# Two edits to the order of small work in a fused attention and rational feed-forward kernel: later normalisations, and stores and broadcasts issued ahead of weight transfers

## The chip, the core and the metric

The kernel runs on one core of one Trainium2 chip. The metric is the device time of one launch in microseconds (us), as the median of several runs. TensorE is written PE in the profile, its weight loads PEld; VectorE is DVE, ScalarE is ACT, GpSimd is POOL, and SyncE, which issues nearly all DMAs here, is SP.

## The reference

Attention over 4 batches and 8 heads with 576 positions and head size 64, with a learned bias on the distance of two positions, and then a feed-forward layer whose activation is a rational function. Cut to what matters:

```python
scores = scale * np.matmul(q, k.transpose(0, 1, 3, 2))
scores = scores + bias.transpose(2, 0, 1)[None, :, :, :]
scores = scores - np.max(scores, axis=-1, keepdims=True)
attn = np.exp(scores)
attn = attn / (np.sum(attn, axis=-1, keepdims=True) + 1e-09)
x = np.matmul(attn, v)                      # to 2304 tokens x 512
h = x @ w_in                                # 512 -> 2048
g = P(h) / (Q(h) + 1e-06)                   # two polynomials in h and |h|
return g @ w_out                            # 2048 -> 512
```

## The kernel before, in words

The work is done in two stages, and their instructions are put in order by hand: each engine executes what the program gives it in the order of the program, and the framework only adds the waits. That holds for SP too: a DMA whose wait isn't over holds up all DMAs behind it.

**Attention.** There are 16 units, a pair of heads of one batch each: unit u is pair u // 4 of batch u % 4. After a start in which the bias table is built, 72 steps handle 128 query rows (or, for the last 64 rows of two neighbouring units, a shared step) each, two steps to a round: round r (`rnd`, line 589) starts steps 2r and 2r + 1 and goes on with the steps of the rounds before. Within a round the order is:

- at the start, SP issues loads (`loads`), and DVE copies an output block of an earlier step from PSUM into the unit's tile `xs` (`puts`, line 494), then does the first part of a weights job;
- PE does the scores of both steps (`product`, line 340). DVE adds the bias and finds the maximum (`e_ttr`, line 356), ACT takes the exponential (line 372);
- PE transposes the probabilities of the two steps before (line 416), ACT copies them out (line 431), and PE multiplies them by v (line 485). The sums of the rows are collected on the way, and `put_tails` stores them to the DRAM tensor `rs` (lines 455 and 460);
- at the round's end stand the parts of the weights job that come last, the stores of finished units (line 402), the loads of the sums' reciprocals (line 388) and further loads.

**Normalisation.** The output of a unit is collected in `xs` without its division. The sums go to DRAM and come back as a broadcast over 64 partitions for each head, two DMAs into the tile `rb` (`load_rb`, line 385). `e_norm` (line 393) makes the multiply of the 128x576 tile (line 400), for most units on POOL, and the store to the DRAM tensor `xd` (line 402), which runs at the end of the round of the multiply. The tiles have few buffers: `rb` two and `xs` four, so that unit u + 2's broadcast waits for unit u's multiply, and unit u + 4's first copy into `xs` for unit u's store. `done_to` (line 533) says when a unit is due, by e, the step by which its last sums are under way (twice the round in which they go to DRAM): its broadcast is issued when step e is done with, and its multiply joins the list `norms` some steps later (line 542). A round takes one entry of that list, if one of its two POOL slots is free (lines 607 to 610): the slot `pool` ahead of the score passes, or `pool2` behind the second of them.

**Weights.** Beside the attention, 20 jobs split the weights into a high and a low part (`w_conv`, line 135, by the schedule of `job_plan`, line 559): a load of `wx` (line 139), DVE, ACT and POOL work (line 176 a POOL copy, line 180 a DVE join that waits for it, line 187 a POOL subtraction), and stores (lines 127 and 195). Two jobs take three rounds: the first of them fills `pool`, the second `pool2`, the third both, which are the rounds divisible by 3.

**Second stage.** From about 277 us on, the feed-forward runs over five tiles of tokens, twice, each half of the hidden size in turn. It reads the attention's output back from `xd` (`load_x`, line 284).

Of the kernel before, what the change touches and what calls it, by code (L numbers as in the profile page):

```python
# [37 lines left out]
def tile_attn_moe(  # L38
# [193 lines left out]
    with tc.manual_schedule():  # L232
# [3 lines left out]
        with ExitStack() as actx:  # L236
# [14 lines left out]
            def load_bias(p, c):  # L251
                if p not in bias:
                    bias[p] = bpool.tile([P, 10, S], F32, tag="bias", name=f"bias{p}")
                t = bias[p]
                r0, r1 = tab_rows(c, 2 * p), tab_rows(c, 2 * p + 1)
                for o, x, y, r in ((5 + c, 0, S, r1[:, 0:S]), (c, 64, S, r0[:, 0:512]), (c, 0, 64, r0[:, 512:S])):
                    n = P if c < 4 else 64
                    for z in range(0, P, n):
                        nc.sync.dma_start(out=t[z:z + n, o, x:y], in_=r)

            def load_qk(u, eng=nc.sync):
                p, b = units[u]
                t = qkp.tile([P, 2, S], F32, tag="qk", name=f"qk{u}", bufs=3)
                eng.dma_start(out=t, in_=qkt[b, p])
                qk[u] = (t[:, 0], t[:, 1])

            def load_v(u, eng=nc.sync):
                p, b = units[u]
                t = vpool.tile([P, 5, P], F32, tag="v", name=f"v{u}")
                eng.dma_start(out=t, in_=vp[b, p])  # L270
                vt[u] = t
# [4 lines left out]
            def load_x(n_, t, k0=0, k1=KD):  # L276
                if k0 == 0:
                    xr[n_] = xps[0].tile([P, KD, TM], F32, tag="xr", name=f"xr{n_}")
                x = xr[n_]
                d = 0  # L280
                while d < TS[t]:
                    b, o = divmod(T0[t] + d, S)
                    w = min(TS[t] - d, S - o)
                    nc.sync.dma_start(out=x[:, k0:k1, d:d + w], in_=xd[b][:, k0:k1, o:o + w])
                    d += w
# [40 lines left out]
            def side(i):  # L326
                return 4 * ((i // 2 - 1 + i) % 2) if i > 1 else 4
# [57 lines left out]
            def load_rb(u):  # L385
                t = rb[u] = npool.tile([P, S], F32, tag="rb", name=f"rb{u}")
                for j in range(2):
                    nc.sync.dma_start(
                        out=t[64 * j:64 * j + 64],
                        in_=rsum[u // 2][u % 2, j:j + 1, :].to_broadcast([64, S]),  # L390
                    )

            def e_norm(u):
                x = xs.pop(u)
                p, b = units[u]
                eng = V if u in (NX, NU - 1) else G
                f = rb.pop(u)

                def part(a, z):
                    op = eng.tensor_tensor(out=x[:, a:z], in0=x[:, a:z], in1=f[:, a:z], op=ALU.mult)  # L400
                    if z == S:
                        stores.append(lambda: nc.sync.dma_start(out=xd[b][:, p, :], in_=x))
                    return op

                return [lambda: part(0, S)]
# [59 lines left out]
            def weave(first, second):  # L465
                t = [0, 0]
                rest = [list(first), list(second)]
                while rest[0] or rest[1]:
                    r = int(not rest[0] or (bool(rest[1]) and t[1] < t[0]))
                    ns, op = rest[r].pop(0)  # L470
                    t[r] += ns
                    op()
# [28 lines left out]
            NS = len(steps)  # L501
            NU = len(units)
# [8 lines left out]
            def loads(i):  # L511
                g, c = divmod(i, UPG)
                for u, x, y in ((2 * g + 2, 0 if g else 4, 3 if g else 6), (2 * g + 3, 5 if g else 7, 8)):
                    if u < NU and c == x:
                        load_qk(u)
                    if u < NU and c == y and u != 3:
                        load_v(u)
                if i == UPG + 2:
                    load_v(3)
                p, r = divmod(i, 2 * UPG)  # L520
                r = {2: 0, 7: 1, 11: 2, 13: 3, 16: 4}.get(r)
                if r is not None and p + 1 < NP:
                    load_bias(p + 1, r)
                if i == NS - 18:
                    load_x(0, 0, 0, KD - 1)
                if i == NS - 5:
                    load_x(1, 1, 0, KD - 1)
# [5 lines left out]
            def done_to(k):  # L533
                for u in range(NU - 1):
                    e = 2 * full[u]
                    if k == (e if u < NX else e - 2):
                        load_rb(u)
                    if u == NX:
                        if k == NS - 8:
                            x12.append(xs[u])  # L540
                            late.extend(e_norm(u))
                    elif k == (NS if u == NU - 2 else min(e + 2 + u % 2 * 2, NS - 3)):
                        norms.extend(e_norm(u))

            def run(todo):
# [3 lines left out]
            def behind(x, y):  # L549
                tc.add_manual_dep(x.ins, y.ins.name, ORDER, reason="one at a time")  # L550
# [5 lines left out]
            def ended(*ks):  # L556
                return [steps[k][0] for k in ks if k >= 0 and last_of(k)]
# [31 lines left out]
            def rnd(r):  # L589
                i = 2 * r  # L590
                plan = job_plan(r)
                loads(i)
                op = None
                while puts:
                    op = puts.pop(0)()
                for x in plan["first"]:
                    op = x()
                for x in plan["act"]:
                    x()
                us = ended(i - 4, i - 3)  # L600
                sa, sb = e_qk(i), e_qk(i + 1)
                b, o = side(i), side(i + 1)
                ZZ = (o + 1, o + 3)
                main, ends, adds, copy = e_tp(i - 2, (b, b + 1), ZZ, us)
                main_, ends_, _, copy_ = e_tp(i - 1, (b + 2, b + 3), ZZ)
                weave(sa[0] + sb[0], sa[1] + sb[1])
                for k in ("pool", "pool2"):
                    if not plan[k] and norms:
                        plan[k].append(norms.pop(0))
                        break  # L610
                for x in plan["pool"]:
                    x = x()
                    if op is not None:
                        behind(x, op)
                e_ttr(i, 0, True)
                op = e_ttr(i, 1)
                for x in plan["between"]:
                    op = x()
                run(late)
                for x in plan["pool2"]:  # L620
                    behind(x(), op)
                small = [ends[r] + ends_[r] + adds[r] for r in range(2)]
                weave(main[0][:4] + small[0] + main[0][4:] + main_[0], main[1] + small[1] + main_[1])
                copy(1, 2)
                copy(0, 1)
                copy_(0, 2)
                for j in range(2):
                    e_ttr(i + 1, j)
                put_tails(i - 2, 2, ZZ, us)
                put = e_pv(i - 3, b + 1) if i > 2 else None  # L630
                puts.append(e_pv(i - 2, b))
                hi = split_x(0, (i - NS + 12) // 2) if i in (NS - 12, NS - 10, NS - 8) else ()
                if i == NS - 4:
                    hi = split_x(0, KD - 1, x12[0][:, :TS[0]])
                for x in hi[:1]:
                    x()
                for k in (i, i + 1):
                    for j in range(2):
                        e_exp(k, j)
                recip(i - 2)  # L640
                recip(i - 1)
                if put:
                    put()
                for x in plan["last"] + list(hi[1:]):
                    x()
                run(stores)
                done_to(i - 2)
                done_to(i - 1)
                loads(i + 1)
                if r == 2:  # L650
                    for x in jobs[:4]:
                        x[0]()
# [37 lines left out]
            with ExitStack() as bctx:  # L690
# [62 lines left out]
                for y, n in enumerate(order):  # L753
# [9 lines left out]
                    for a, z in zip(cuts, cuts[1:]):  # L763
                        b = pa[a // 512]
                        o = W[:, b, a % 512:a % 512 + z - a]
                        for c in range(4):
                            x = rows[n, c]
                            x = x[:, a - mid:z - mid] if a >= mid else x[:, mid - a:mid - z:-1]
# [4 lines left out]
                    e = rpool.tile([P, EW], F32, tag="e", name=f"e{n}")  # L773
# [9 lines left out]
                    g, k = divmod(n, 8)  # L783
# [310 lines left out]
```

## Time and profile before

| what | us |
| --- | --- |
| median of 3 runs | 660.6 (660.6 to 661.12) |
| the profiled execution | 661.6 |
| its span, first to last instruction | 659.8 |
| PE busy | 652.1 |
| DVE busy | 563.1 |
| ACT busy | 470.8 |
| POOL busy | 153.8 |

Times in the rows are microseconds from the start of the span. A row of the timeline gives the start, the length, the engine, the line, the operation and its tiles, the number of instructions that are merged in it, and in brackets the idle time of the engine ahead of it with what ended it. A q behind an engine's name means its sequencer, which issues DMAs. Busy shares are averages over stages with different limits; what a change is worth is read from the place where it acts.

### The profile page before, as it was taken

How to read it: one execution, taken by the hardware profiler on the slowest of the kernel's cores; microseconds unless marked ns; L12 is line 12 of the kernel's file. 1: busy time of each engine (PE TensorE's matmuls, PEld its weight loads, DVE VectorE, ACT ScalarE, POOL GpSimd, SP SyncE). 2: the span in 40 equal slices, each digit the busy share in tenths (PEclk: the TensorE clock that was granted, in tenths of full speed). 3: DMA queues.
4: the chain of work that ended last, by engine and by line, in shares of the span. 5: the costliest groups of instructions: out<-in, count | busy, mean ns of one | idle time of the engine just before them, and what ended most of it. 6: DMA issues, size and time to landing. Idle time of an engine off the chain costs nothing.

```text
span 659.8 us, 16141 instructions
## 1 busy us (share of the span) xinstructions
PE 652.1 (99%) x6276; PEld 549.6 (83%) x6276; DVE 563.1 (85%) x1102; ACT 470.8 (71%) x757; POOL 153.8 (23%) x108
## 2 busy tenths in 40 slices
PE   9999999999999999999999999999999999999997
PEld 7767888888888788988888888989988888888996
DVE  7997889998889895899999989979769779687776
ACT  7978999999899897767667566576655555555551
POOL 1000234333333331122222221222221221212211
PEclk9999999999999999999999999999999999999999
DMA  6899599788787674452835607669431301312031
GB/s 248 302 329 323 159 289 303 255 280 265 240 305 252 218 259 126 138 188 71 261 98 171 226 19 256 211 203 321 142 111 49 129 0 66 110 43 85 1 113 48
DMA packets 69901, 118.98 MB, mean 180 GB/s; under 512 B 9024, under 2 KB 30912, under 8 KB 69824
## 3 DMA queue, kind: packets, MB, share of 16 engines
q1 hardware_dynamic: 69680, 117.78, 53.9%
q8 instruction: 49, 0.80, 0.5%
q14 instruction: 28, 0.23, 0.1%
q10 hardware_dynamic: 144, 0.16, 0.1%
HBM read 79.17 MB, written 35.61 MB: 174 GB/s over the span
## 4 chain that ended last, share of the span: by engine, by line
PE 89%; DMA 4%; DVE 2%; ACT 2%; issue 1%; SPq 0%; POOL 0%; DVEq 0%; POOLq 0%
PE ps L313 30%; PE ps L922 30%; PE ps L485 10%; PE ps L340 9%; PE ps L769 6%; PE ps L416 5%; ACT p L372 1%; DMA rb<-rs 1%; DVE s L356 1%; DMA wx<-in_w_out_dram 1%; DMA ws<-wl 1%; ACT pt L431 1%; DVE ring L741 0%; DMA cst<-in_cst_dram 0%; POOL wl L187 0%
## 5 line engine op out<-in xcount | busy, mean ns | idle before, releaser
L892 POOL TENSOR_TENSOR gl<-m,r 128x1024 fp32r<-128x1024 f32 (+1 forms) x39 | 85.6, 2194 | 299.4 <-DVE m L885 262.3
L843 ACT ACTIVATE w<-ps,babs 128x1024 f32<-128x1024 f32 (+1 forms) x40 | 41.2, 1031 | 107.9 <-PE ps L313 104.2
L372 ACT ACTIVATE p<-s,m 128x576 f32<-128x576 f32 x144 | 110.1, 781 | 0.6 <-DVE m L356 0.6
L356 DVE CUSTOM_DVE_ANT_0 s<-ps,bias 128x576 f32<-128x576 f32 (+1 forms) x144 | 95.1, 681 | 6.8 <-PE ps L340 2.1
L431 ACT COPY pt<-ps 128x512 f32<-128x512 f32 (+1 forms) x109 | 71.7, 732 | 17.8 <-PE ps L416 17.8
L922 PE MATMUL ps<-woh,gh 128*128 128x512 f32 x216 | 84.3, 390 | 0.0
L922 PE MATMUL ps<-wol,gh 128*128 128x512 f32 x216 | 84.3, 390 | 0.0
L340 PE MATMUL ps<-qk 64*128 64x288 f32 (+1 forms) x640 | 81.7, 418 | 0.0
L855 DVE SCALAR_TENSOR_TENSOR u<-w,babs,ps 128x1024 f32<-128x1024 f32 (+1 forms) x40 | 46.9, 1172 | 38.2 <-ACT t L844 38.1
L485 PE MATMUL ps<-pt,v 128*64 128x128 f32 (+1 forms) x1280 | 78.5, 266 | 0.8 <-ACT pt L431 0.5
L485 PEld LDWEIGHTS ps<-pt,v 128*64 128x64 f32 x1280 | 65.3, 137 | 5.8 <-ACT pt L431 1.8
L313 PE MATMUL ps<-xb,wih 128*128 128x512 f32 (+1 forms) x240 | 68.8, 368 | 0.0
L850 ACT ACTIVATE u<-u 128x1024 f32<-128x1024 f32 (+1 forms) x40 | 39.1, 978 | 40.1 <-DVE u L855 40.0
L340 PEld LDWEIGHTS ps<-qk 64*128 64x128 f32 (+1 forms) x640 | 51.0, 176 | 19.5 <-issue 5.8
L416 PEld LDWEIGHTS ps<-ident,p 64*128 64x128 f32 x1296 | 50.3, 138 | 6.2 <-DVE m L356 0.5
L871 DVE SCALAR_TENSOR_TENSOR gh<-t,cst,r 128x1024 fp32r<-128x1024 f32 (+1 forms) x40 | 46.9, 1173 | 9.3 <-ACT r L852 6.9
L922 PE MATMUL ps<-woh,gl 128*128 128x512 f32 x216 | 53.8, 389 | 0.0
L416 PE MATMUL ps<-ident,p 64*128 64x64 f32 x1296 | 51.1, 226 | 0.1
L878 DVE SCALAR_TENSOR_TENSOR m<-u,qc,gh 128x1024 f32<-128x1024 f32 (+1 forms) x40 | 47.1, 1178 | 4.0
L313 PEld LDWEIGHTS ps<-xb,wih 128*128 128x128 f32 x240 | 44.6, 188 | 6.1
L885 DVE SCALAR_TENSOR_TENSOR m<-t,cst,m 128x1024 f32<-128x1024 f32 (+1 forms) x40 | 47.1, 1178 | 1.4
L864 DVE SCALAR_TENSOR_TENSOR t<-t,cst,ps 128x1024 f32<-128x1024 f32 (+1 forms) x40 | 47.0, 1174 | 1.4
(84 smaller groups left out, 1344.7 us busy)
## 6 DMA issues: line engine op xcount, KB each, us to landing
tab<-e SPq DMA_DIRECT2D x36, 295.5 KB
qk<-in_qkt_dram SPq DMA_DIRECT2D x16, 576.0 KB
wx<-in_w_in_dram SPq DMA_DIRECT2D x16, 512.0 KB
wx<-in_w_out_dram SPq DMA_DIRECT2D x16, 512.0 KB
v<-in_vp_dram SPq DMA_DIRECT2D x16, 320.0 KB
ws<-wh SPq DMA_DIRECT2D x20, 256.0 KB
ws<-wl SPq DMA_DIRECT2D x20, 256.0 KB
bias<-tab SPq DMA_DIRECT2D x16, 288.0 KB
```

The lines of the kernel that those rows point to most:

```text
L313: on(T.matmul(hps[s][:, j, :w_], w[:, k, sl], x[:, k, :w_], start=(k == 0 and z == 0), stop=(k == KD - 1 and z == 2),), b + j)
L340: on(T.matmul(W[o, b, :SH], q[r, x], k[r, a * SH:(a + 1) * SH], start=True, stop=True), b)
L356: op = on(V.tensor_tensor_reduce(out=t3[:, a], in0=W[:, b:b + 2][:, a, :SH], in1=b3[:, a], scale=-0.125, scalar=least, op0=ALU.add, op1=AL ...
L372: A.activation(out=prob[i][:, z * S:z * S + S], in_=t, func=AF.Exp, bias=m, scale=-1.0, accum_out=sums[u % 4][:, k:k + 1],)
L416: on(T.transpose(W[:, b, o:o + 64], src[x, :], ident[x, x]), b)
L431: on(A.copy(out=t.rearrange("p x (r s) -> p r x s", r=2)[:, a:z], in_=W[:, to[a]:to[a] + z - a].rearrange("p r (x s) -> p r x s", s=64),), ...
L485: on(T.matmul(ps[y, o], vt[n][:, kc, y], w_, start=(kc == 0), stop=(kc == 4)), b, mem=(f"pt{i % 3}", f"tl{i // 2 % 2}"))
L864: on(V.scalar_tensor_tensor(out=rt[s, "t"], in0=rt[s, "t"], scalar=abs_[:, 1:2], in1=hp(s), op0=ALU.add, op1=ALU.mult,), *hb(s), mem="t")
L878: V.scalar_tensor_tensor(out=m, in0=rt[s, "u"], scalar=qc, in1=rt[s, "gh"].bitcast(F32), op0=ALU.add, op1=ALU.mult,)
L885: V.scalar_tensor_tensor(out=m, in0=rt[s, "t"], scalar=abs_[:, 0:1], in1=m, op0=ALU.add, op1=ALU.subtract)
L892: eng.tensor_tensor(out=lo, in0=rt[s, "m"], in1=rt[s, "r0"], op=ALU.mult)
L922: on(T.matmul(po[n, c], l[:, j, c * P:(c + 1) * P], r[fp][:, j, :], start=(first and x is a), stop=(last and x is z),), OB[c])
```

## The change

Two edits. The first sets one due time for all normalisations that go through the common branch: e + 4, where units with an even number had e + 2 and units with an odd number e + 4. The second changes the order of calls at a round's end: the stores of finished units, then the broadcasts and due lists of `done_to`, and only then the last parts of the weights job.

```diff
--- before.py
+++ after.py
@@ -539,7 +539,7 @@
                         if k == NS - 8:
                             x12.append(xs[u])
                             late.extend(e_norm(u))
-                    elif k == (NS if u == NU - 2 else min(e + 2 + u % 2 * 2, NS - 3)):
+                    elif k == (NS if u == NU - 2 else min(e + 4, NS - 3)):
                         norms.extend(e_norm(u))
 
             def run(todo):
@@ -641,11 +641,11 @@
                 recip(i - 1)
                 if put:
                     put()
-                for x in plan["last"] + list(hi[1:]):
-                    x()
                 run(stores)
                 done_to(i - 2)
                 done_to(i - 1)
+                for x in plan["last"] + list(hi[1:]):
+                    x()
                 loads(i + 1)
                 if r == 2:
                     for x in jobs[:4]:
```

## Rows read from the trace of the kernel before

**Rows 1.** The page: engines' busy time, granted clock by slices, the chain that ended last

```profile
PE 652.1 (99%) x6276; PEld 549.6 (83%) x6276; DVE 563.1 (85%) x1102; ACT 470.8 (71%) x757; POOL 153.8 (23%) x108
...
PEclk9999999999999999999999999999999999999999
...
PE 89%; DMA 4%; DVE 2%; ACT 2%; issue 1%; SPq 0%; POOL 0%; DVEq 0%; POOLq 0%
```

**Rows 2.** The timeline of the ends of rounds 8 and 9, rounds 10 and 11

```profile
99.23 0.54 SPq L402 DMA_DIRECT2D xd<-xs  x1
...
101.55 0.46 SPq L139 DMA_DIRECT2D wx<-in_w_out_dram  x1
...
102.10 1.48 SPq L388 DMA_DIRECT2D rb<-rs  x2
...
103.64 1.53 SPq L259 DMA_DIRECT2D bias<-tab  x3
...
104.56 1.41 POOL L400 TENSOR_TENSOR xs<-xs,rb 128x576 f32<-128x576 f32 x1 [0.81 <-DVE m L356]
...
106.73 0.65 SPq L455 DMA_DIRECT2D rs<-rt  x1
...
107.58 2.37 PE L340 MATMUL ps<-qk 64*64 64x288 f32 x24
...
107.75 0.29 DVE L494 COPY xs<-ps 128x128 f32<-128x128 f32 x1 [0.19 <-issue]
...
108.71 0.79 PEld L340 LDWEIGHTS ps<-qk 64*128 64x128 f32 x8 [0.44 <-DVE wk L155]
...
113.45 2.21 PE L340 MATMUL ps<-qk 64*128 64x288 f32 x16
```

**Rows 3.** The timeline of round 20, with the broadcast issued ahead of it

```profile
153.87 1.68 SPq L388 DMA_DIRECT2D rb<-rs  x2
...
160.06 2.37 PE L340 MATMUL ps<-qk 64*64 64x288 f32 x24
...
162.63 1.41 POOL L400 TENSOR_TENSOR xs<-xs,rb 128x576 f32<-128x576 f32 x1 [4.17 <-DMA rb<-rs]
...
162.66 1.93 DVE L180 SCALAR_TENSOR_TENSOR wm<-wm,wh 128x512 uint32<-128x512 uint32 x1
...
166.77 2.21 PE L340 MATMUL ps<-qk 64*128 64x288 f32 x16
```

**Rows 4.** Line 180 over the whole span: count, least, median and longest ns

```profile
L180 DVE SCALAR_TENSOR_TENSOR wm<-wm,wh x20: 685/686/1932, 75.3 to 241.0; 128x512 uint32<-128x512 uint32 x20
```

**Rows 5.** The timeline of round 30

```profile
219.25 2.21 PE L340 MATMUL ps<-qk 64*128 64x288 f32 x16
...
219.62 1.42 POOL L400 TENSOR_TENSOR xs<-xs,rb 128x576 f32<-128x576 f32 x1 [7.84 <-DMA rb<-rs]
...
222.33 1.04 POOL L176 COPY wm<-wx 128x1024 uint16<-128x1024 uint16 x1
...
223.40 0.69 DVE L180 SCALAR_TENSOR_TENSOR wm<-wm,wh 128x512 uint32<-128x512 uint32 x1 [1.46 <-POOL wm L176]
...
225.70 0.34 PE L485 MATMUL ps<-tl,v 128*64 128x64 f32 x4 [1.22 <-DVE tl L443]
...
226.55 2.21 PE L340 MATMUL ps<-qk 64*128 64x288 f32 x16
```

**Rows 6.** The timeline of SP near the end of the attention, queue nearly empty

```profile
255.90 0.42 SPq L460 DMA_DIRECT2D rs<-rt  x1
257.22 1.11 SPq L388 DMA_DIRECT2D rb<-rs  x2
```

**Rows 7.** The windows: engines' busy us (count), granted clock, DMA share, GB/s

```profile
100.00:125.00 25.00, 24.95 (x434) 21.59 (x430) 22.61 (x78) 23.54 (x51) 9.47 (x8) 1.00 0.90 304
```

**Rows 8.** Line 720, the first matmuls, up to 4.6 us and from 4.8 us

```profile
L720 PE MATMUL ps<-warm x16: 421/422/582, 1.1 to 4.4; 128*128 128x128 f32 x16
...
L720 PE MATMUL ps<-warm x5: 274/276/421, 4.4 to 5.0; 128*128 128x128 f32 x5
```

## The prediction, made before the changed kernel was seen

> **What bounds the kernel now.** I read the page first, then the windows, then the timeline round by round. The page shows TensorE busy for 652.1 of 659.8 us, with 90% or more of its clock granted in every slice, and the chain that ended last is 89% TensorE [rows 1]. So nothing that the change does to DVE, ACT, POOL or the DMA queue counts by itself; it counts where TensorE waits for it, and only there. The attention rounds between 45 and 250 us are a strict beat: a round begins where the scores' matmuls (line 340) begin, and the plain one from 107.58 to 113.45 takes 5.87 us [rows 2]. Two rounds break the beat, and both by way of a normalisation on POOL. In round 20 the broadcast of unit 6's sums was issued at 153.87 to 155.55 and the multiply that reads it started only at 162.63; the DVE instruction of line 180 that started 0.03 us later took 1.93 us instead of its median 0.69, and the round took 166.77 - 160.06 = 6.71 us [rows 3, 4]. In round 30 unit 10's multiply, due in round 29, had waited 7.84 us for its broadcast; the weights' copy behind it on POOL started at 222.33, line 180 on DVE waited 1.46 us for that, TensorE 1.22 us behind it, and the round took 226.55 - 219.25 = 7.30 us [rows 5]. The reader should see in both that POOL is nearly idle and does harm only by being late.
>
> **Edit one, the due time (line 542).** Even units become due at e + 4 instead of e + 2, one round later; odd ones stay. A due normalisation is taken in the next round that leaves a POOL slot free, one each round, and rounds divisible by 3 leave none (both slots belong to weights). Worked through line 533 to 610: unit 0 goes from round 8 to 10, unit 1 from 10 to 11 (it queues behind unit 0), unit 2 from 11 to 13, 4 from 16 to 17, 6 from 20 to 22, 8 from 25 to 26, 10 from 29 to 31; the rest stay. The same 14 POOL multiplies run, so no busy time is added. What goes: both harmful ones now come two rounds after the old place, with the broadcast long landed. Round 20 gives back 6.71 - 5.87 = 0.84 us and round 30 gives 7.30 - 5.87 = 1.43 us, together 2.3 us. Next late would be DVE and ACT, but other rounds with a multiply in the same slot show that they keep the 5.87 us beat [rows 2].
>
> A later multiply also frees two buffers later, and this is the edit's price. The broadcast tile has two buffers: unit 2's broadcast, issued on SP at the end of round 9, needs unit 0's multiply done, which now is in round 10. SP issues in order, so everything behind that broadcast stands. The unnormalised output has four buffers: unit 4's first copy from PSUM (line 494, DVE, first thing in round 11) needs unit 0's store landed; that store was issued at 99.23 and is now issued at the end of round 10. I went through all later units: each has at least one round (5.8 us) between its store and the copy that wants the buffer, and unit 12's broadcast follows unit 10's multiply of the same round. Only round 11 collides.
>
> **Its size.** In round 10 the slot after the second score pass runs its multiply at 104.56, 1.41 us long, done at 105.97 [rows 2]; today that is unit 1's, then unit 0's. Only then does SP go on. With the lengths of today's rows it issues the two broadcasts 1.48, the next weights 0.46, three bias loads 1.53, the sums of unit 3 0.65: 4.12 us, to 110.1; then the store, 0.54 like today's, to 110.6 [rows 2]. Nothing shows a store's landing, so I bound it. Below: an unloaded issue that ended at 256.32 had landed when the broadcast that needs it was issued at 257.22, 0.9 us [rows 6]. Above: unit 6's broadcast needed 162.63 - 155.55 = 7.1 us under load [rows 3]. The queue will have run dry before 106, but then takes 1.7 MB in one burst (two 144 KB broadcasts, 512 KB, 576 KB, 4 KB, the store's 288 KB, by the shapes in the code); at the 304 GB/s of this stretch [rows 7] that alone is 5.6 us from 106, plus 0.9 twice: 113.4. I take the middle of the bounds, 4.0 us, as the byte count lies between: landed at 114.6, ends 111.5 and 117.7. The copy that ran at 107.75 starts there, 6.85 us late, and behind it on DVE stand the weights' mask and all score passes of the round. TensorE is no cover: half of the round's scores go to the bank that this copy empties, and it waited for DVE there already, 0.44 us until 108.71 [rows 2]. I allow 0.25 us for what it can still do: 6.6 us of stall, ends 3.2 and 9.7.
>
> **The clock behind the stall.** No row of before has TensorE idle for longer than about 1.2 us once at work, and that did not lower the granted clock [rows 1, 5]. The only rows after a long rest are the first: from 1.05 to about 4.6 us each 128x128 matmul took 0.42 us, with starts 0.21 us apart, then 0.28 us, starts 0.11 us apart: the 1.2 and the 2.4 GHz level [rows 8]. If the stall drops the clock, I expect the same again: some 3.6 us at half speed, 1.8 us lost; ends 0 and twice that. I take 1.8, as a rest of 6.6 us is nearer to the start's rest than to 1.2 us. The Trainium skill (TensorE: Matmul & The Clock Gate, "Part 1: The HAM clock gate") says that the half-rate clock is the default and that TensorE falls back to it after a stretch without work, which speaks against a change that opens such a hole. By that rule the result is 666.7 us, without it 664.9; no row here shows a fall in mid-kernel.
>
> **Edit two, the order at a round's end (lines 641 to 648).** Only SP's order changes: the DVE instructions among the moved calls have none of their own engine to pass. The store (one DMA) and the broadcast (two) go ahead of the weights' store or load. Where nothing waits that is worth at most the weights' issue, 0.3 to 1 us earlier for a transfer that now has two rounds to spare: nothing, hidden by that slack. Its price if the broadcast waits is that the weights' transfers stand behind it. In round 9 that is the load of job 7, wanted in round 14; in rounds 31 and 33, where the broadcast waits for its own sums, the last weights' stores, wanted in the second stage. All have whole rounds of cover: nothing. It also takes the high part's store out from in front of unit 0's store; that is why I didn't count it above.
>
> **Sum.** 6.6 + 1.8 - 2.3 = 6.1 us slower. The profiled execution took 661.6 us around its span of 659.8, 0.15% over the median of 660.6, so on the median: 666.7 us.
>
> **Rivals.** (a) *The stall is there and the clock stays up*: 660.6 + 6.6 - 2.3 = 664.9 us. For it: the clock never left full once it was reached [rows 1]. Against: it was never tried by such a rest. (b) *Faster: unit 0's store lands in time*. Place: round 11, DVE's first copy. It decides at 107.75: if SP did not stand at unit 2's broadcast, the store could be issued when the multiply ends, 105.97, take 0.54 and land 0.9 later, 107.4. Then only the 2.3 us count: 658.3 us. Against: two buffers, and a third broadcast ahead of the first one's reader in program order. (c) *The beat does not come back*: the moved multiplies meet line 180 elsewhere, as in round 20, and the 2.3 us are not gained: 669.0 us. Against: line 180's median of 0.69 us over 20 runs [rows 4] says that such a meeting is the exception. (d) *The stall is short*, near its lower end with no clock loss: 660.6 + 3.2 - 2.3 = 661.5 us, no change.
>
> **How the numbers follow.** Forecast 0.55, (a) 0.20, (b) 0.13, (c) 0.05, (d) 0.07. About 0.2%, 1.3 us, can be told from no change; so faster 0.13, same 0.07, slower 0.80. The forecast's own ends are 661.5 and 671.5 (9.7 + 3.6 - 2.3 = 11.0). The range leaves out (b), most of (d) and the last microsecond above: 662.0 to 670.5.
>
> **What would show it.** Round 11 lengthened by 6 to 9 us, with a DVE wait before the copy of line 494 that ends with the store of unit 0, and line 340 waiting on DVE; SP standing for some 5 us at line 388 until POOL's multiply ends near 106; a granted clock of half behind it; rounds 20 and 30 back to 5.8 to 5.9. I am wrong if round 11 keeps its beat, or if line 400 on POOL still waits some microseconds for a broadcast in rounds 20 to 31.

## The result, and the profile after

The changed kernel takes 667.78 us (667.56 to 668.59), the kernel before beside it 660.74 us: a ratio of 1.0108, with a 95% interval from 1.0090 to 1.0125, so 7.0 us slower. The forecast was 666.7 us, within 662.0 to 670.5. The two profiled executions differ by 6.0 us in their spans (665.8 and 659.8).

The page of the changed kernel has the same work and nearly the same busy times as [rows 1]; what is new is one slice in which TensorE falls to six tenths and the granted clock to eight:

```profile
PE 654.1 (98%) x6276; PEld 550.0 (83%) x6276; DVE 561.6 (84%) x1102; ACT 470.6 (71%) x757; POOL 153.5 (23%) x108
...
PE   9999996999999999999999999999999999999997
...
PEclk9999998999999999999999999999999999999999
```

It is the seventh of 40, from 99.9 to 116.5 us, and the place is round 11. Its timeline, which answers to [rows 2] line by line:

```profile
101.77 0.49 SPq L264 DMA_DIRECT2D qk<-in_qkt_dram  x1
...
104.75 1.41 POOL L400 TENSOR_TENSOR xs<-xs,rb 128x576 f32<-128x576 f32 x1 [0.81 <-DVE m L356]
...
106.19 1.15 SPq L388 DMA_DIRECT2D rb<-rs  x2
...
107.38 0.59 SPq L139 DMA_DIRECT2D wx<-in_w_out_dram  x1
...
107.76 1.20 PE L340 MATMUL ps<-qk 64*64 64x288 f32 x16
...
108.01 2.21 SPq L259 DMA_DIRECT2D bias<-tab  x3
...
110.32 0.65 SPq L455 DMA_DIRECT2D rs<-rt  x1
...
111.01 0.39 SPq L402 DMA_DIRECT2D xd<-xs  x1
...
114.73 0.29 DVE L494 COPY xs<-ps 128x128 f32<-128x128 f32 x1 [6.99 <-DMA xd<-xs]
...
115.08 1.46 PEld L340 LDWEIGHTS ps<-qk 64*128 64x128 f32 x8 [6.62 <-DVE xs L494]
115.08 2.29 PE L340 MATMUL ps<-qk 64*128 64x288 f32 x8 [6.12 <-DVE xs L494]
...
117.16 2.13 PE L416 MATMUL ps<-ident,p 64*128 64x64 f32 x36
...
121.76 2.21 PE L340 MATMUL ps<-qk 64*128 64x288 f32 x16
...
123.80 1.42 PE L416 MATMUL ps<-ident,p 64*128 64x64 f32 x36
```

It reads like a chain. POOL's multiply, now unit 0's, ends at 106.16. SP, which had ended its last issue at 102.26, only then issues unit 2's broadcast, and behind it all that had gathered: weights, bias, sums. Unit 0's store is issued at 111.01, where it was at 99.23 before. DVE's first copy of unit 4 has waited 6.99 us for it. TensorE has done the first step's scores (16 instructions, 1.20 us), needs the bank that this copy empties, and stands 6.1 us. Then its work takes longer: the 36 transposes 2.13 us against 1.42 us a round later. The windows (busy us of PE, PEld, DVE, ACT, POOL, then the granted clock, DMA share, GB/s) show why:

```profile
101.97:107.76 5.79, 5.79 (x96) 5.02 (x94) 5.24 (x18) 5.62 (x13) 2.45 (x2) 1.00 0.78 280
...
113.00:119.60 6.60, 4.52 (x48) 3.74 (x50) 4.37 (x14) 2.06 (x4) 2.70 (x2) 0.50 0.60 204
...
121.76:127.63 5.87, 5.87 (x115) 5.19 (x113) 4.77 (x17) 4.66 (x12) 2.32 (x2) 1.00 0.80 263
```

The granted clock is at full up to the stall, at half (1.2 GHz) from 113 to 119.6 us, and at full again in the next round. Round 11 takes 121.76 - 107.76 = 14.0 us instead of 5.87.

The rounds that should gain did. TensorE's timeline has round 20 at 174.24 - 168.36 = 5.88 us, against 6.71 [rows 3], and round 30 at 232.59 - 226.72 = 5.87 us, against 7.30 [rows 5]:

```profile
168.36 2.37 PE L340 MATMUL ps<-qk 64*64 64x288 f32 x24
174.24 1.97 PE L340 MATMUL ps<-qk 64*128 64x288 f32 x14
...
226.72 2.21 PE L340 MATMUL ps<-qk 64*128 64x288 f32 x16
232.59 1.73 PE L340 MATMUL ps<-qk 64*128 64x288 f32 x12
```

So the spans add up: 8.1 us lost in round 11, 0.8 and 1.4 won, 0.2 lost at the start, together 6.1 of 6.0 us.

### The profile page after: what moved, and what is told of

It reads as the page before. It is cut to its first block, busy times and chain, and to the rows that moved or that the text cites. A ratio compares the mean times of both kernels' runs of the same rounds, so it can differ in the third digit from the quotient of the medians.

```text
span 665.8 us, 16141 instructions
## 1 busy us (share of the span) xinstructions
PE 654.1 (98%) x6276; PEld 550.0 (83%) x6276; DVE 561.6 (84%) x1102; ACT 470.6 (71%) x757; POOL 153.5 (23%) x108
## 4 chain that ended last, share of the span: by engine, by line
PE 95%; ACT 2%; issue 1%; SPq 1%; DMA 1%; POOL 0%; DVE 0%; DVEq 0%; POOLq 0%
PE ps L313 30%; PE ps L922 30%; PE ps L485 12%; PE ps L340 11%; PE ps L769 6%; PE ps L416 6%; ACT p L372 1%; PE ps L720 1%; ACT pt L431 1%; DMA xd<-xs 1%; SPq L259 0%; POOL xs L400 0%; SPq L388 0%; DVE pre L943 0%; SPq L455 0%
```

## The experiments

My theory: the whole price lies in one place, unit 0's late multiply, by way of SP and the buffers of two tiles; the gain lies in late multiplies of units 6 and 10 and is worth having by itself. The rivals: the new order on SP costs, or later multiplies cost in general, or SP's standing costs by itself.

**One edit at a time.** The due time alone:

```diff
-                    elif k == (NS if u == NU - 2 else min(e + 2 + u % 2 * 2, NS - 3)):
+                    elif k == (NS if u == NU - 2 else min(e + 4, NS - 3)):
```

> The due time alone, with the old order at a round's end. My theory, that unit 4's first copy in round 11 waits for unit 0's store and that this store stands behind unit 2's broadcast on SP: round 11 takes 13.5 to 14.6 us, rounds 20 and 30 are plain at 5.8 to 5.9, the time is 667.5 to 668.5 us. Rival, that the new order on SP is what costs: no long round, 658 to 660 us.

Measured: 667.82 us, ratio to before 1.0101 (1.0086 to 1.0117). Round 11 takes 121.43 - 107.77 = 13.7 us; the store is issued at 110.45, as the load of the weights had gone out before SP stood. The due time is the whole loss.

The order alone (stores and `done_to` ahead of the last weights' parts, old due times):

```diff
-                for x in plan["last"] + list(hi[1:]):
-                    x()
                 run(stores)
                 done_to(i - 2)
                 done_to(i - 1)
+                for x in plan["last"] + list(hi[1:]):
+                    x()
```

> The order alone, with the old due times. My theory: round 11 plain, since unit 0 is normalised in round 8 as before; the broadcasts of units 6 and 10 are issued 0.5 to 2 us earlier and land ahead of the weights' load, so that round 20 loses most of its 0.84 us over the beat and round 30 at least half of its 1.43 us: 658.4 to 659.8 us. Rival, that the order is what costs: 664 us or more.

Measured: 660.42 us, ratio 0.9983 (0.9969 to 0.9998): a gain just clear of none, and a time above the range that I gave. Round 11 is plain. Round 20 is plain, as unit 6's multiply now starts 0.9 us into the round; round 30 too, and round 29 takes 5.95 us. I had priced this edit at nothing beside the other. Alone it does what it can be read to do: unit 6's broadcast is issued ahead of the 512 KB load (152.42 against 153.59) and has landed when its multiply starts. That is one profiled execution; whether the whole gain comes from there isn't shown.

**One unit at a time.** The changed kernel with unit 0 alone at its old due time:

```diff
-                    elif k == (NS if u == NU - 2 else min(e + 4, NS - 3)):
+                    elif k == (NS if u == NU - 2 else min(e + (4 if u else 2), NS - 3)):
```

> The changed kernel with unit 0 alone back at its old due time. My theory: unit 0 is multiplied in round 8, SP does not stand, round 11 is plain at 5.8 to 5.9 us, clock at full, and the 2.3 us of rounds 20 and 30 stay won: 658.3 us, give or take 0.6. Rival, that the later multiplies of other units (1, 2, 4, 8) also cost: 661 us or more, with another long round.

Measured: 660.08 us, ratio 0.9979 (0.9970 to 0.9988). Round 11 is plain, rounds 20 and 30 are won, and of the others only round 26 is longer than in the kernel before, 6.04 us and so 0.2 over the beat. The price is gone; the gain is real but 1.4 us, not 2.3, so that the time lies above the range that I gave.

The kernel before with unit 0 alone late:

```diff
-                    elif k == (NS if u == NU - 2 else min(e + 2 + u % 2 * 2, NS - 3)):
+                    elif k == (NS if u == NU - 2 else min(e + (4 if u % 2 or u == 0 else 2), NS - 3)):
```

> The kernel before with unit 0 alone made late, old order (units 1 and 2 move one slot because they queue behind it). My theory: the whole price of the change sits here: round 11 takes 13.5 to 14.5 us, and 667.9 to 669.2 us, more than the changed kernel since rounds 20 and 30 keep their waits. Rival, that it takes the other late units or the new order too: under 664 us.

Measured: 668.47 us (667.42 to 670.35), ratio 1.0112 (1.0092 to 1.0133). One unit's due time makes the whole loss: round 11 takes 121.67 - 107.87 = 13.8 us. In its profile, round 30 keeps its wait and is even longer, 234.21 - 226.60 = 7.61 us, by the same chain as in [rows 5]:

```profile
226.60 2.21 PE L340 MATMUL ps<-qk 64*128 64x288 f32 x16
227.28 1.41 POOL L400 TENSOR_TENSOR xs<-xs,rb 128x576 f32<-128x576 f32 x1 [8.13 <-DMA rb<-rs]
...
231.06 0.69 DVE L180 SCALAR_TENSOR_TENSOR wm<-wm,wh 128x512 uint32<-128x512 uint32 x1 [1.75 <-POOL wm L176]
...
234.21 2.21 PE L340 MATMUL ps<-qk 64*128 64x288 f32 x16
```

But round 20, whose multiply is at its old place too, takes 5.88 us here: the multiply started 0.45 us after line 180 (171.31 against 170.86) and not ahead of it, and line 180 took its usual 0.69 us. That loss isn't in every run.

The kernel before with units 6 and 10 alone moved:

```diff
-                    elif k == (NS if u == NU - 2 else min(e + 2 + u % 2 * 2, NS - 3)):
+                    elif k == (NS if u == NU - 2 else min(e + (4 if u % 2 or u in (6, 10) else 2), NS - 3)):
```

> The kernel before with two units alone moved, 6 and 10, old order. My theory: these two are the whole gain: rounds 20 and 30 at 5.8 to 5.9 us, 658.4 us, give or take 0.6. Rival, that the gain needs the new order or the other units: at most half of it, 659.6 us or more.

Measured: 659.68 us, ratio 0.9980 (0.9971 to 0.9989). The two units alone bring the whole gain that any version here brings, with rounds 20 and 30 plain, so it needs neither the new order nor the other units. But it is 1.3 us, and the time is above my range and where I had put the rival's. The profiled execution, at 660.97 us the slowest of the 11, shows that other rounds can lose as much: rounds 8 and 11, plain in the profile of before, take 6.2 and 6.5 us in this one. Its timeline:

```profile
92.44 1.42 POOL L400 TENSOR_TENSOR xs<-xs,rb 128x576 f32<-128x576 f32 x1 [5.93 <-DVE m L356]
...
93.03 1.38 DVE L180 SCALAR_TENSOR_TENSOR wm<-wm,wh 128x512 uint32<-128x512 uint32 x1
...
110.55 1.41 POOL L400 TENSOR_TENSOR xs<-xs,rb 128x576 f32<-128x576 f32 x1 [3.98 <-DMA rb<-rs]
...
110.77 1.73 DVE L180 SCALAR_TENSOR_TENSOR wm<-wm,wh 128x512 uint32<-128x512 uint32 x1
```

It is the meeting of [rows 3] again, at other places: a multiply that starts a little ahead of line 180 holds it up. In the second of them the row names the broadcast as what the multiply waited for. In the first it names DVE's line 356, so there a late broadcast isn't shown as the cause.

**Which wait.** Two buffers are involved, and each can be given one more, in a pool that lives through the attention only. First a place of its own for unit 4's output, so that its copy waits for no store:

```diff
-                        xs[x] = npool.tile([P, S], F32, tag="xs", name=f"xs{x}", bufs=4)
+                        xs[x] = (apool if x == 4 else npool).tile([P, S], F32, tag="xs", name=f"xs{x}", bufs=1 if x == 4 else 4)
```

> The changed kernel with a buffer of its own for unit 4's output, so that its first copy waits for no store. My theory: SP still stands at unit 2's broadcast until unit 0's multiply ends near 106 us, but nobody waits for that; round 11 plain at 5.8 to 5.9 us, clock at full, 659.5 to 660.6 us like the run with unit 0 early. Rival, that SP's standing itself is the price, by weights and loads that come late: 663 us or more.

Measured: 659.63 us, ratio 0.9979 (0.9970 to 0.9988). The timeline shows SP standing as before and the store as late as before, and nobody minds:

```profile
106.17 1.11 SPq L388 DMA_DIRECT2D rb<-rs  x2
107.73 2.37 PE L340 MATMUL ps<-qk 64*64 64x288 f32 x24
...
111.20 0.39 SPq L402 DMA_DIRECT2D xd<-xs  x1
...
113.60 2.21 PE L340 MATMUL ps<-qk 64*128 64x288 f32 x16
```

Round 11 is 113.60 - 107.73 = 5.87 us. So what is behind SP had cover enough, as the prediction had it; the one wait that counts is that of the copy for the store.

Then a place of its own for unit 2's broadcast, so that SP does not stand:

```diff
-                t = rb[u] = npool.tile([P, S], F32, tag="rb", name=f"rb{u}")
+                t = rb[u] = (apool if u == 2 else npool).tile([P, S], F32, tag="rb", bufs=1 if u == 2 else 2, name=f"rb{u}")
```

> The changed kernel with a buffer of its own for unit 2's broadcast, so that SP does not stand; unit 4's copy still waits for unit 0's store. My theory: the store is issued near 107.6 instead of 111.0 us and lands 3 to 4 us later, the copy waits some 3.5 us instead of 7.0, TensorE some 3 us, round 11 takes 8.5 to 9.5 us, and the time is 662 to 664 us. Rival, that the late multiply alone sets the store: round 11 stays at 13.5 to 14 us and 667.8 us.

Measured: 664.95 us, ratio 1.0057 (1.0044 to 1.0071), and round 11 11.3 us: between the theory and its rival, and outside the range that I gave. The rows show where:

```profile
107.71 0.32 SPq L402 DMA_DIRECT2D xd<-xs  x1
107.77 1.20 PE L340 MATMUL ps<-qk 64*64 64x288 f32 x16
...
112.26 0.29 DVE L494 COPY xs<-ps 128x128 f32<-128x128 f32 x1 [4.50 <-DMA xd<-xs]
...
112.60 1.24 PE L340 MATMUL ps<-qk 64*128 64x288 f32 x8 [3.63 <-DVE xs L494]
...
119.08 2.21 PE L340 MATMUL ps<-qk 64*128 64x288 f32 x16
```

The store was issued where I expected it, at 107.71. It let the copy go only 4.2 us after its issue ended (112.26 against 108.03); with SP standing it took 3.3 us (114.73 against 111.40). While SP stood, the DMA engines ran out of work in part, and behind that they were full again. The windows of the changed kernel have the DMA engines busy for 0.41 of the time from 107 to 108 us and all the time (1.02) from 110 to 111, just before its store was issued; the last one is its wait for the store (the last two columns are the DMA share and GB/s):

```profile
107.00:108.00 1.00, 1.00 (x20) 0.80 (x20) 0.74 (x2) 1.00 (x3) 0.00 (x0) 1.00 0.41 139
110.00:111.00 1.00, 0.00 (x0) 0.00 (x0) 0.00 (x0) 0.00 (x0) 0.00 (x0) 1.00 1.02 343
111.40:114.73 3.33, 0.00 (x0) 0.00 (x0) 0.00 (x0) 0.00 (x0) 0.00 (x0) 0.72 1.05 336
```

In this run they were at work throughout:

```profile
107.00:108.00 1.00, 1.00 (x20) 0.81 (x20) 0.76 (x2) 1.00 (x3) 0.00 (x0) 1.00 0.98 272
108.03:112.26 4.23, 0.94 (x16) 0.31 (x8) 0.00 (x0) 1.78 (x6) 0.00 (x0) 1.00 0.98 331
```

The rates of the two waits are alike, 336 and 331 GB/s. By my estimate from them 1.1 MB moved between the store's issue and the copy with SP standing, and 1.4 MB here. That fits a longer queue ahead of the store in this run, but no row says which bytes stood ahead of it.

The clock fell here too: the windows have it at 0.50 from 114.15 to 117.56, after TensorE had stood for 3.6 us. SP's standing is worth 667.8 - 665.0 = 2.8 us of the price (2.7 by the spans); the late multiply alone costs the rest.

**The clock.** 24 matmuls are added to the changed kernel where TensorE would stand, into PSUM columns that are free then:

```diff
-                weave(sa[0] + sb[0], sa[1] + sb[1])
+                if r == 11:
+                    weave(sa[0], sa[1])
+                    for _ in range(24):
+                        on(T.matmul(W[:, 6, SH:SH + P], ident, ident, start=True, stop=True), 6)
+                    weave(sb[0], sb[1])
+                else:
+                    weave(sa[0] + sb[0], sa[1] + sb[1])
```

> The changed kernel with 24 extra 128x128 matmuls on TensorE in round 11 between the scores of its two steps, some 5.3 us at the full clock, into a part of PSUM that is free there; the output is not touched. They run while TensorE would wait for unit 4's copy. My theory, that 1.5 us of round 11 are work at the half clock behind the stall: the granted clock stays at full through round 11, which takes 12.3 to 12.8 us instead of 14.0, and the time is 666.0 to 666.6 us. Rival, that those 1.5 us are DVE and ACT catching up and not the clock: 667.5 us or more.

Measured: 666.39 us, ratio 1.0078 (1.0064 to 1.0092), with more work on TensorE than the changed kernel. Timeline and window of round 11 (the row of line 609 counts each added matmul twice):

```profile
107.83 1.20 PE L340 MATMUL ps<-qk 64*64 64x288 f32 x16
...
108.96 5.62 PE L609 MATMUL ps<-ident 128*128 128x128 f32 x48
...
114.79 0.29 DVE L494 COPY xs<-ps 128x128 f32<-128x128 f32 x1 [6.97 <-DMA xd<-xs]
...
115.13 1.24 PE L340 MATMUL ps<-qk 64*128 64x288 f32 x8 [0.55 <-DVE xs L494]
...
120.23 1.00 PE L340 MATMUL ps<-qk 64*128 64x288 f32 x6
```

```profile
107.83:120.23 12.40, 11.77 (x151) 10.19 (x149) 5.30 (x17) 5.74 (x13) 2.69 (x2) 1.00 0.70 233
```

The copy waits as long as ever, 6.97 us. The eight score instructions behind it take 1.24 us instead of 2.29, the clock stays at full, and the round takes 12.4 us instead of 14.0. The half clock costs 1.6 us.

## Why the prediction was right, and where it was off

**The place and the chain: right.** Round 11, DVE's copy, the store of unit 0, SP at unit 2's broadcast until POOL's multiply ends near 106. The single-unit runs show that the whole loss hangs on unit 0, and the extra output buffer takes it away. That all other units have a round to spare was right as well: with unit 0 early no round is more than 0.2 us over the beat. One sign was mis-sized: SP stood for 3.9 us (102.26 to 106.19) and not some 5.

**The stall: 6.6 us expected, 6.1 to 6.6 measured** (matmuls and weight loads). The copy was put at 114.6 and ran at 114.73. That the middle of two wide ends came so close is in part luck, as two errors cancel: SP's issues took until 111.4 instead of 110.6 (above all the bias loads, 2.21 us instead of 1.53), the landing 3.3 us instead of 4.0. The lower end was added up wrong: 111.5 - 107.75 - 0.25 is 3.5 us and not 3.2, so that rival (d) would be 661.8 us and the forecast's own ends 661.8 and 671.6. The measured time lies well inside either way.

**The clock: 1.8 us expected, 1.6 measured.** That it falls was right. That the size is near is again partly luck: TensorE worked 4.5 us at the half clock (115.08 to 119.6) and not 3.6, but lost 1.6 us by it and not half of that time. The start was also a weaker stand-in than the prediction says. Its half level was read from the distance of the matmuls alone, while the window of the same stretch has the granted clock at full:

```profile
1.00:4.50 3.50, 3.45 (x16) 3.45 (x17) 0.76 (x3) 1.49 (x3) 0.96 (x8) 1.00 0.77 229
```

In round 11 the granted clock itself shows the fall. The clock fell after a rest of TensorE, as the Trainium skill has it (TensorE: Matmul & The Clock Gate, "Part 1: The HAM clock gate"); the windows agree, at 0.50 behind rests of 6.1 and 3.6 us and at 1.00 in the run whose added matmuls filled the rest. Rival (a) falls.

**The gain: 2.3 us expected, 1.3 to 1.4 measured.** This is the term that was mis-sized: I took the whole excess of both long rounds of one profiled execution, 661.6 us, off a median of 660.6, as if every execution had it. Multiplies in rounds 8, 11 and 20 meet line 180 in some executions and not in others; of the two profiles with unit 6 at its old place in the old order (before, and unit 0 alone late), one shows round 20 long, and the wait of round 30 differs too, 1.43 and 1.74 us over the beat. The kernel before spreads: of its 27 runs beside the due time, the order, unit 0 early and units 6 and 10, 24 lie between 659.8 and 662.1 us, the 11 runs with unit 0 early between 659.64 and 660.34. From profile to profile most of the gain is there: the span with unit 0 early is 657.9 us against 659.8. But the median of the 27 runs is 661.43, only 0.2 us under the profiled execution, so that the choice of the execution doesn't explain the whole shortfall. Which rounds a median execution loses time in is not shown, and that part of the cause stays open. The sum with the sizes found is 6.6 + 1.6 - 1.3 = 6.9 us, against 7.0 measured.

**The order: nothing expected, nothing measured in this company** (667.82 us without it, 667.78 with it), but 1.1 us won alone (0.0017 of 661.4 us). The profiles fit one reading: late multiplies and early broadcasts cure the same wait, so that the second of them finds nothing left.

Rival (b) falls by the timeline, (c) by rounds 20 and 30 and by line 180, which in the changed kernel's profile never takes more than 0.69 us, (d) by the size. Which version is best can't be told: the three fastest (units 6 and 10 alone, the extra output buffer, unit 0 early) lie at 0.9980, 0.9979 and 0.9979, some 0.2% faster than the kernel before, and the order alone at 0.9983 lies within their intervals.

## What to carry to other kernels

A reader that is moved later also frees its buffer later: go through every buffer that it or its successor holds, write down who wants each next and in which queue that one stands, and look at the first units most closely, where the distances are not yet the steady ones. A rule for all units made simpler can be wrong for a single one, and one unit was the whole price here. Of a single profile take the waits, but their sum only after a look at how the runs spread around it.

## What the hardware showed beside that

Line 180 on DVE and the multiply on POOL, each with both inputs in SBUF, do not run at once. Where the multiply starts first, line 180 ends 0.54 to 0.55 us behind the multiply's end in all five cases that the traces of the two kernels and the experiments hold: 164.59 against 164.04 by [rows 3], 94.41 against 93.86 and 112.50 against 111.96 above, and, with less overlap, 93.59 against 93.04 in the kernel before and 216.95 against 216.40 with the order alone. So what is left of its 0.69 us is pushed back nearly whole. Where line 180 starts first, it takes 0.69 us as ever and the multiply, 1.41 us as a rule, ends 1.28 us behind it in all three such cases, as in round 11 of the kernel before:

```profile
110.18 0.69 DVE L180 SCALAR_TENSOR_TENSOR wm<-wm,wh 128x512 uint32<-128x512 uint32 x1
...
110.38 1.77 POOL L400 TENSOR_TENSOR xs<-xs,rb 128x576 f32<-128x576 f32 x1 [4.40 <-DVE m L356]
```

That round keeps the beat, and so does round 20 with unit 0 alone late, where the multiply gives way in the same manner. It costs the kernel nothing there, where POOL has time to spare, and 0.8 us in round 20 of the kernel before, where DVE is the one that waits. The Trainium skill gives the rule (SBUF — State Buffer, "SBUF: two separate sides"): the port pair that both share is a lock, held for a whole instruction by whichever starts first. The rows agree.

A store's landing isn't a constant. The same store let the copy go 3.3 us after its issue ended when SP had stood, and 4.2 us after it when SP had not, so that SP's standing paid back 0.9 us of what it took.
